# Keys of the third half by token tiles: DMA transposes and halving extrema in place of TensorE transposes and reductions, in a fused attention and feed-forward kernel

## The chip, the cores and the metric

The kernel runs on one core of a Trainium2 chip. The metric is device time in microseconds. Before the change three runs gave a median of 269.87 us (269.5 to 270.08). Engines are called TensorE (PE; its weight loads PEld), VectorE (DVE), ScalarE (ACT), GpSimd (POOL) and SyncE (SP, which only issues DMAs here).

## The reference, cut to what matters

```python
# q, k, v: (4, 8, 768, 64) float32; chunk = 32, nc = 24, top_k = 6
k_min, k_max = min / max of k over each chunk of 32 keys
ub = sum_d maximum(q * k_min, q * k_max)          # bound of each query for each chunk
ub = where(causal by chunk, ub, -1e9)
sel = the 6 chunks of largest ub, per query
scores = where(sel and causal, q @ k.T / 8, -1e9)
attn = softmax(scores) @ v                         # -> x: (3072, 512)
out = square(relu(x @ w_in)) @ w_out               # w_in (512, 2048), w_out (2048, 512)
```

## The kernel before

The sequence of each of the four batches is cut into two halves of 384 tokens, and `ORDER = ((0, 0), (1, 0), (0, 1), (1, 1), (2, 0), ...)` gives the eight (batch, half) groups, called halves 0 to 7 here; the change concerns index 2, the third, which is the second half of batch 0. Each half has four slots, one for each pair of heads, numbered s = 0 to 31; the third half is slots 8 to 11. All engine queues follow the order of the program text (a manual schedule), and each engine takes its instructions strictly in that order.

For a slot, `step_P` brings keys and queries into the form with the head dimension on partitions, `step_U` computes the chunk bounds on TensorE (tile `ub`) and picks the six largest on VectorE (MAX8, L375), `step_V` moves the choice into the code rows of the queries (transposes `qt`, copies L425), `step_E` computes scores (`ps`, L438), exponentials on ScalarE (`e`, L444) and the causal cut on GpSimd (L448), and `step_F` multiplies by v (`po`, L464), normalizes (`x`, L474) and sends x through a DMA transpose to `xT` (L478). Between these steps, `f1` takes pieces of the feed-forward of an earlier half out of a queue: up-projections (`ph`, L544, then `ht` on ScalarE and `h` on VectorE) and down-projections (`py`, L560).

There are two ways in which keys and queries are brought in.

- On TensorE, for halves 0 to 2 (`ON_PE = 3`). `load_packed` brings four tokens to a partition row in one DMA for each of k and q. `step_T` makes eight TensorE transposes for the keys of a slot (`tk`) and eight for its queries (`tq`) into PSUM. `step_T2` then has `relus_T` on ScalarE, `extrema` on VectorE (two reductions over 384 keys, L221 and L222, and one product with `hmask` into `kbd`, L223), and `place`, which copies keys (VectorE, two copies, L283) and queries (ScalarE) into `kqs`, from which the scores read.
- By DMA, for halves 3 to 7. `load_n` brings token tiles, three DMAs of 128 tokens for each of k and q. `tr` issues a DMA transpose of one tile from SP into `kqT`, `place_dma` two DMAs from there into `kqs`, and `step_K` gives six parts for VectorE that find minima and maxima of all four slots by halving (16, 8, 4, 2, 1; L326) and multiply by `hmask` (two products for each, L332). The parts are taken one at a time by `k1` at fixed places of the slot loop.

Loads are put at the ends of slots by `at(s, ...)` and drained by `go`, all on GpSimd's queue. At the ends of slots 2 to 4 stand the packed k and q of the third half, the first half of `w_out`, codes, and the second half of `w_out`. `first` and `by_sp` hold what SP issues at the start of a slot and after `step_F`.

Of the kernel before, what the change touches and what calls it, by code (L numbers as in the profile page):

```python
# [16 lines left out]
HT = 3  # L17
# [10 lines left out]

ORDER = ((0, 0), (1, 0), (0, 1), (1, 1), (2, 0), (2, 1), (3, 0), (3, 1))

ON_PE = 3

TP = 4
PP = HB // TP
# [5 lines left out]
def kernel(  # L40
# [9 lines left out]
    nc = tc.nc  # L50
# [3 lines left out]
    NP = H // 2  # L54
# [160 lines left out]
    st = {}  # L215

    def extrema(kt, s):
        b, half, p = slots[s]
        km = work.tile([128, 2, 12], BF16, tag="km", name="km")
        kv = kt.rearrange("r (j c e) -> r c j e", j=TP, c=12)  # L220
        nc.vector.tensor_reduce(km[:, 0, :], kv, axis=AX.XY, op=ALU.min)  # L221
        nc.vector.tensor_reduce(km[:, 1, :], kv, axis=AX.XY, op=ALU.max)  # L222
        nc.vector.tensor_mul(  # L223
            kbds[b % 2][:, p, :, :, 12 * half:12 * half + 12], hmask,
            km.unsqueeze(2).to_broadcast([128, 2, 2, 12]))
# [5 lines left out]
    def by_token(x):  # L231
        return x.rearrange("r (p j) -> r p j", j=TP)
# [7 lines left out]
    def step_T(s, kp, qp, ns="kq"):  # L240

        b, half, p = slots[s]
        t = st.setdefault(s, {})
        for n in ns:
            pool, tag = kp if n == "k" else qp
            x = t[n] = pool.tile([128, HB], BF16, tag=tag, name="t" + n)
            if n == "q" and s < NP:
                for hh in range(2):
                    for j in range(HT):
                        nc.tensor.matmul(  # L250
                            x[D * hh:D * hh + D, 128 * j:128 * (j + 1)],
                            lhsT=qn0[:, j, p, hh, 0:D],
                            rhs=ident, is_transpose=True, start=True, stop=True)
                continue
            for hh in range(2):
                for j in range(TP):
                    nc.tensor.matmul(
                        x[D * hh:D * hh + D, PP * j:PP * j + PP],
                        lhsT=packed(n, s // NP)[:, 2 * p + hh, D * j:D * j + D],
                        rhs=ident[0:PP, 0:PP], is_transpose=True, start=True, stop=True)  # L260

    def step_T2(s):
        relus_T(s)
        extrema(st[s]["k"], s)
        if s >= NP:
            place(s, "k", nc.vector.tensor_copy)
            place(s, "q", nc.scalar.copy)

    def relus_T(s):
# [10 lines left out]
    def place(s, n, copy, h0=0, h1=2):  # L280
        b, half, p = slots[s]
        for h in range(h0, h1):
            copy(by_token(kqs[b % 2][0:D, p, 2 * half + "kq".index(n), h, :]),  # L283
                 in_order(st[s][n][D * h:D * h + D]))
# [54 lines left out]
    F, Y, A = (psF, "ph"), (psY, "py"), (psA, "att")  # L339

    S_ = (psS, "ps")

    def step_P(s):
        if s // NP >= ON_PE:
            relus(s)
            return
        step_T(s, *((S_, Y) if s == NP + 1 else (F, Y) if s < NP + 2 else
                    (Y, S_) if s < 2 * NP + 1 else (S_, A)))
        if s >= NP + 2 and s != 2 * NP + 1:
            step_T2(s)  # L350

    def step_U(s):
# [20 lines left out]
        for j in range(j0, HT):  # L373
            for hh in range(2):
# [3 lines left out]
            (qn0[:, j0:, p, :, D:D + ncs] if s < NP else  # L378
             chosen[s % 2][:, j0:, :, 0:ncs] if s < ON_PE * NP else
             nsel[half][:, s % 2, :, j0:, 1, 0:ncs].rearrange("p h j c -> p j h c")),  # L380
# [197 lines left out]
    first = {}  # L578

    def at(s, fn, *a):  # L580
        later.setdefault(s, []).append(lambda: fn(*a))
# [15 lines left out]
        at(0, load_w_in, 1024 * g, 1024 * g + 1024)  # L597
    for j in range(HT):
        at(1, load_vt, 1, j)
    for n in "kq":  # L600
        at(2, load_packed, n, 2)
    at(4, codes, 0, 1, nc.gpsimd.dma_start)
    for g in range(2):
        at(3 + g, load_w_out, 8 * g, 8 * g + 8)
# [9 lines left out]
    by_sp = {}  # L614
    for g in range(4, 2 * B):
        for i in range(2 * HT):
            at(4 * g - (7 if g == 4 else 8) + i // HT, load_n, "kq"[i // HT], g, i % HT)
    s0 = 4 * ON_PE - 3
    for i in range(2 * HT):
        first.setdefault(s0 + i // HT, []).append((tr, ON_PE, "kq"[i // HT], i % HT))  # L620
# [80 lines left out]
    parts = []  # L701
# [5 lines left out]
    for s, (b, half, p) in enumerate(slots):  # L707
        if s < NP:
            continue
        hb = s // NP  # L710
        nb = len(BANKS[half])
        hf = nb // 2
        quota = [((4, 4, 4, 4) if hb == 1 else (8, 6, 7, 7))[p]]
        for fn, *a in first.get(s, ()):
            fn(*a)
        if (hb == ON_PE - 1 and p == 2) or (ON_PE < hb < 2 * B - 1 and p == 0):
            parts.extend(step_K(hb + 1))

        def f1():
            if quota[0] and queue:  # L720
                quota[0] -= 1
                fill(1, True)

        if s == NP:
            for n in range(hf):
                step_E(s, 0, n)
            step_F(s - 1, 0)
            step_F(s - 1, 1)
            step_P(s + 1)
            relus_T(s + 1)  # L730
            x_T(0, 1, F, (0,))
            x_copy(0, 1, 0, 1, nc.vector.tensor_copy)
            busy(8, *A)
            x_T(0, 1, F, (1,))
            x_copy(0, 1, 1, 2, nc.vector.tensor_copy)
            push(0)
            extrema(st[s + 1]["k"], s + 1)
            place(s + 1, "k", nc.vector.tensor_copy)
            place(s + 1, "q", nc.scalar.copy)
        if s == 2 * NP:  # L740
            for n in range(hf):
                step_E(s, 0, n)
            relus_T(s + 1)
            place(s + 1, "q", nc.scalar.copy)
            step_F(s - 1, 0)
            step_F(s - 1, 1)
            push(1)
            f1()
            f1()
            extrema(st[s + 1]["k"], s + 1)  # L750
            place(s + 1, "k", nc.vector.tensor_copy)
        if p == 0 and hb > 2:
            step_F(s - 1, 0)
            step_F(s - 1, 1)
            push(hb - 1)
        else:
            f1()
        if s > NP and s != 2 * NP:
            for n in range(hf):
                step_E(s, 0, n)  # L760
        k1()
        f1()
        if p == 0 and hb > 2:
            f1()
            f1()
        if hb > 1 and s != 2 * NP:
            f1()
        if hb < ON_PE:
            go(s, 2)
        for n in range(hf, nb):  # L770
            step_E(s, 0, n)
        if hb < ON_PE and p:
            k1()
        if s < NS - 2 or s + 1 == 3 * NP:
            step_U(s + (1 if hb < ON_PE else 2))
        if s + 1 == ON_PE * NP:
            step_W(s + 1)
        if hb >= ON_PE and s < NS - 2:
            step_W(s + 2)
        if ON_PE * NP - 2 <= s <= ON_PE * NP - 1:  # L780

            nc.vector.memset(
                nsel[1 - s % 2][:, :, :, :, 1, :]
                .rearrange("p i h j c -> p (i h j) c"), 0.0)
        late_f = half == 0 and hb > 2
        border = p == 0 and hb > 1
        if not border and not (late_f and p == NP - 1):
            f1()
        if p and s > NP:
            step_F(s - 1, 0)  # L790
            step_F(s - 1, 1)
        for fn, *a in by_sp.get(s, ()):
            fn(*a)
        if half == 0 and not (late_f and p in (0, NP - 1)):
            f1()
        if hb < ON_PE and p:
            k1()
        for n in range(hf):
            step_E(s, 1, n)
            if border and half and n == 0:  # L800

                f1()
        if not (late_f and p == 0):
            f1()
        if s + 1 == ON_PE * NP:
            step_P(s + 2)
            step_Q(s + 2)
        if s + 1 < ON_PE * NP:
            step_V(s + 1)
        if hb == ON_PE and p == 0:  # L810
            parts.extend(step_K(hb + 1))
        k1()
        if hb < ON_PE:
            go(s, 99)
        for n in range(hf, nb):
            step_E(s, 1, n)
        if hb >= ON_PE:
            go(s, 99)
        k1()
        if hb == ON_PE - 1 or (hb == ON_PE and p):  # L820
            k1()
        if s + 1 < ON_PE * NP:
            step_P(s + 2)
            if s + 2 == ON_PE * NP:
                step_Q(s + 2)
        if s + 1 == ON_PE * NP:
            f1()
            step_U(s + 2)
            step_W(s + 2)
        if hb >= ON_PE or s + 1 == ON_PE * NP:  # L830
            if s + 3 < NS:
                step_P(s + 3)
                step_Q(s + 3)
        f1()
        if half == 0:
            f1()
        while quota[0] and queue:
            f1()
# [40 lines left out]
```

## Time and profile before

| | |
|---|---|
| median of three runs | 269.87 us |
| profiled execution | 269.78 us |
| its span | 268.1 us |
| granted TensorE clock | 1.0 in the span's record |
| busy time in the span: TensorE / VectorE / ScalarE / GpSimd | 255.3 / 160.5 / 178.1 / 90.8 us |
| instructions | 6632 |
| bytes read from HBM / written | 27.26 / 6.29 MB |

Times in rows are microseconds from the start of the span unless marked ns. A row of the timeline gives start, length, engine, line, operation, tiles as out<-in, shape and count; brackets at the end name idle time of the engine before it and what ended it. A row by stretch gives the stretch, its length, the busy time (and count) of PE, PEld, VectorE, ScalarE and GpSimd, the granted clock, the DMA share and GB/s. Rows of the DMA view give queue (q0: the loads that GpSimd issues; q1: what SP issues), packets, MB and share; or an issue with its count, KB and the median time to landing. "SPq" marks a DMA issue on SP.

### The profile page before, as it was taken

Reading aid. Unit: us, or ns where it says so; the run is one execution under the profiler, and the core shown is the slowest. Engines: PE = TensorE matmul, PEld = TensorE weight load, DVE = VectorE, ACT = ScalarE, POOL = GpSimd, SP = SyncE. Lnnn points to the kernel's source line nnn. Section 1 sums busy time; section 2 is a strip of 40 time slices with the busy share of each in tenths; the row PEclk is TensorE's granted clock in tenths of the full one; section 3 lists DMA queues with packets and bytes.
Section 4 is the critical chain, followed back from the end, with each engine's and each line's share of the span. In section 5 each row is a group of like instructions: output and inputs, shape, how many; then the busy total and the mean of one; then the engine's idle time right before and its main releaser. Section 6 shows DMA issues by size and latency. Waiting matters only on the chain.

```text
span 268.1 us, 6632 instructions
## 1 busy us (share of the span) xinstructions
PE 255.3 (95%) x2436; PEld 157.4 (59%) x2436; DVE 160.5 (60%) x617; ACT 178.1 (66%) x399; POOL 90.8 (34%) x135
## 2 busy tenths in 40 slices
PE   7878998999999999999999999999999999999995
PEld 6566565556665566655665566745565666645543
DVE  6777999756996458546875576555863233413411
ACT  4887898688976578845575777935685688515500
POOL 8696347426911425235521543310121111000000
PEclk9999999999999999999999999999999999999999
DMA  7999999999998699999994999995532320111112
GB/s 138 153 207 211 181 218 191 120 112 151 131 170 140 137 170 149 117 177 148 191 143 118 130 166 152 157 149 134 128 98 64 61 46 16 57 39 39 39 42 78
DMA packets 116769, 33.98 MB, mean 127 GB/s; under 512 B 103680, under 2 KB 112672, under 8 KB 116736
## 3 DMA queue, kind: packets, MB, share of 16 engines
q0 software_dynamic: 64592, 13.83, 67.2%
q1 hardware_dynamic: 51200, 19.33, 37.8%
q10 hardware_dynamic: 944, 0.39, 0.6%
q8 instruction: 19, 0.31, 0.5%
q14 instruction: 14, 0.11, 0.2%
HBM read 27.26 MB, written 6.29 MB: 125 GB/s over the span
## 4 chain that ended last, share of the span: by engine, by line
PE 76%; DVE 14%; ACT 5%; issue 2%; DMA 1%; SPq 0%; ACTq 0%; DVEq 0%
PE py L560 28%; PE ph L544 24%; PE ps L438 11%; PE po L464 7%; DVE h L550 2%; ACT e L444 2%; PE ub L362 2%; DVE km L326 2%; ACT ht L548 1%; DVE m L375 1%; DMA stage<-in_q_dram 1%; PE py L532 1%; DVE kq L283 1%; DVE x L474 1%; PE idle L637 1%
## 5 line engine op out<-in xcount | busy, mean ns | idle before, releaser
L444 ACT ACTIVATE e<-ps 128x512 bf16<-128x512 f32 x192 | 96.6, 552 | 19.0 <-PE ps L438 17.9
L544 PE MATMUL ph<-xT,w_in 128*128 128x384 bf16 x512 | 98.8, 325 | 0.2 <-ACT ht L548 0.2
L560 PE MATMUL py<-w_out,h 128*128 128x512 bf16 x368 | 87.7, 379 | 0.7 <-ACT ob L566 0.5
L550 DVE TENSOR_TENSOR h<-ht 128x384 bf16<-128x384 bf16 x128 | 46.6, 374 | 56.9 <-ACT ht L548 56.3
L548 ACT ACTIVATE ht<-ph 128x384 bf16<-128x384 f32 x128 | 62.5, 501 | 26.2 <-PE ph L544 25.8
L448 POOL TENSOR_SCALAR_AFFINE_SELECT e<-e 128x384 bf16<-128x384 bf16 x64 | 34.1, 537 | 132.6 <-ACT e L444 132.5
L544 PEld LDWEIGHTS <-w_in 128*128 128x128 bf16 x512 | 47.6, 97 | 30.8 <-issue 1.4
L438 PE MATMUL ps<-kq 96*128 96x384 bf16 (+2 forms) x320 | 57.0, 277 | 1.5 <-DVE kq L414 1.0
L560 PEld LDWEIGHTS <-h 128*128 128x128 bf16 x368 | 34.9, 97 | 36.1 <-issue 1.2
L438 PEld LDWEIGHTS <-kq 96*128 96x128 bf16 x320 | 26.4, 97 | 16.1 <-issue 1.4
L566 ACT COPY ob<-py 128x512 f32<-128x512 f32 x19 | 11.1, 585 | 27.5 <-PE py L560 27.1
L464 PEld LDWEIGHTS <-e 128*128 128x128 bf16 x672 | 25.4, 98 | 4.0
L375 DVE MAX8 m<-ub 128x8 f32<-128x16 f32 (+4 forms) x160 | 16.2, 168 | 18.9 <-PE ub L369 18.5
L464 PE MATMUL po<-vn,e 128*128 128x65 bf16 x672 | 26.6, 194 | 0.0
L474 DVE TENSOR_TENSOR x<-po,r 128x384 bf16<-128x384 f32 x32 | 17.8, 557 | 1.1
L109 POOL DMA_DIRECT2D qn<-in_q_dram x15 | 13.3, 897 | 0.5 <-DVE km L326 0.2
L109 POOL DMA_DIRECT2D kn<-in_k_dram x15 | 13.4, 901 | 0.2
L362 PEld LDWEIGHTS <-qr 128*128 128x128 bf16 x160 | 8.4, 96 | 7.9 <-DVE qr L306 2.2
L326 DVE TENSOR_TENSOR km<-km 128x384 bf16<-128x384 bf16 (+3 forms) x40 | 11.7, 293 | 1.1
L362 PE MATMUL ub<-kbd,qr 128*128 128x48 bf16 (+1 forms) x160 | 9.9, 180 | 2.3 <-DVE kbd L223 0.9
L125 POOL DMA_DIRECT2D vn<-in_v_dram x12 | 10.7, 907 | 0.3 <-issue 0.3
L637 PE MATMUL idle<-ident 128*128 128x128 bf16 x97 | 8.3, 246 | 2.2 <-POOL ident masks.py:199 1.4
(69 smaller groups left out, 177.5 us busy)
## 6 DMA issues: line engine op xcount, KB each, us to landing
out_dram<-ob SPq DMA_DIRECT2D x23, 256.0 KB, 2.5
w_in<-in_moe_w_in_dram POOLq DMA_DIRECT2D x2, 1024.0 KB, 11.8
w_out<-in_moe_w_out_dram POOLq DMA_DIRECT2D x2, 1024.0 KB, 17.8
kn<-in_k_dram POOLq DMA_DIRECT2D x15, 128.0 KB, 5.6
qn<-in_q_dram POOLq DMA_DIRECT2D x15, 128.0 KB, 5.5
kq<-kqT SPq DMA_DIRECT2D x10, 192.0 KB, 3.7
vn<-in_v_dram POOLq DMA_DIRECT2D x12, 128.0 KB, 9.8
vn<-in_v_dram POOLq DMA_DIRECT2D x4, 384.0 KB, 7.9
```

The source lines that it names most:

```text
L109: nc.gpsimd.dma_start(out=nat_of(n, g)[:, DM * j:DM * j + DM].rearrange("p (h d) -> p h d", d=D), in_=rows(n, *ORDER[g], 0, H)[:, 128 * j: ...
L362: nc.tensor.matmul(ub[:, j - j0], lhsT=st[s]["qr"][:, w, 128 * j:128 * (j + 1)], rhs=kbds[b % 2][:, p, w, :, 0:ncs], start=(j == j0 and w ...
L375: nc.vector.max(out=m8[:, j, hh, :], in_=ub[:, j - j0, hh, 0:12 * half + 4 * j + 4])
L438: nc.tensor.matmul(ps[:, at:at + 128 * m], lhsT=kqs[b % 2][0:KR, p, 2 * (j // HT), hh, 128 * (j % HT):128 * (j % HT + 1)], rhs=qc(s, hh)[: ...
L444: nc.scalar.activation(e[:, 512 * n + lo:512 * n + hi], ps[:, lo:hi], ACT.Exp, scale=float(scale))
L448: nc.gpsimd.affine_select(out=d, in_=d, compare_op=ALU.is_ge, fill=0.0, base=0, channel_multiplier=-1, pattern=[[0, 3], [1, 128]])
L464: nc.tensor.matmul(po[:, hh, i, :], lhsT=t["e"][hh][:, c:c + 128], rhs=vn[b % 2][:, 2 * p + hh, j, :], start=(j == 0), stop=(j == iq))
L474: nc.vector.tensor_mul(x[:, p].rearrange("p j (h d) -> p h j d", h=2), po[:, :, :, 0:D], r.to_broadcast([128, 2, HT, D]))
L544: nc.tensor.matmul(ph[:, 0:HB], lhsT=w_in[:, ki, 128 * f:128 * (f + 1)], rhs=xT[:, ki, :], start=(ki == 0), stop=(ki == NKI - 1))
L548: nc.scalar.activation(ht, ph[:, 0:HB], ACT.Relu)
L550: nc.vector.tensor_mul(h, ht, ht)
L560: nc.tensor.matmul(py[t], lhsT=h2[hb, f][:, 128 * t:128 * (t + 1)], rhs=w_out[:, f, :], start=(f == 0), stop=(f == NFI - 1))
```

## The change

The third half's keys take the DMA way; its queries stay on the TensorE way. `K_PE = 2` marks the first half whose keys don't go over TensorE.

- The packed load of these keys becomes three loads of token tiles, one at the end of slot 2 and two at the end of slot 3, behind the packed load of the queries and ahead of `w_out`.
- SP issues three transposes at the start of slot 5, and the two placing DMAs in slot 6.
- The six parts of `step_K(2)` are queued in slot 6, and all are taken before `step_U(8)` in slot 7.
- `step_T` transposes queries alone for slots 8 to 11 (slot 8's into another PSUM bank), and `extrema` and `place` of keys fall away for them.

```diff
 ON_PE = 3
+K_PE = 2
...
-        for n in ns:
+        for n in ns[0 if s < K_PE * NP else 1:]:
...
     def step_T2(s):
         relus_T(s)
-        extrema(st[s]["k"], s)
+        if s < K_PE * NP:
+            extrema(st[s]["k"], s)
+            if s >= NP:
+                place(s, "k", nc.vector.tensor_copy)
         if s >= NP:
-            place(s, "k", nc.vector.tensor_copy)
             place(s, "q", nc.scalar.copy)
...
         step_T(s, *((S_, Y) if s == NP + 1 else (F, Y) if s < NP + 2 else
-                    (Y, S_) if s < 2 * NP + 1 else (S_, A)))
+                    (Y, S_) if s < 2 * NP else (Y, Y) if s == 2 * NP else (S_, A)))
...
-    for n in "kq":
-        at(2, load_packed, n, 2)
+    at(2, load_packed, "q", 2)
+    for j in range(HT):
+        at(2 + (j > 0), load_n, "k", 2, j)
...
+    for j in range(HT):
+        first.setdefault(5, []).append((tr, K_PE, "k", j))
+    by_sp.setdefault(6, []).append((place_dma, K_PE))
...
             f1()
             f1()
-            extrema(st[s + 1]["k"], s + 1)
-            place(s + 1, "k", nc.vector.tensor_copy)
...
+        if hb + 1 == K_PE and p == 2:
+            parts.extend(step_K(K_PE))
         if hb < ON_PE and p:
             k1()
...
         k1()
-        if hb == ON_PE - 1 or (hb == ON_PE and p):
+        if K_PE <= hb + 1 <= ON_PE or (hb == ON_PE and p):
             k1()
```

## The prediction

> **What bounds the kernel now.** I read the page first, then the busy time by stretch, then the chain of waits and each engine's timeline from 24 to 80 us, and last the DMA view over short stretches.
>
> ```profile
> PE 76%; DVE 14%; ACT 5%; issue 2%; DMA 1%; SPq 0%; ACTq 0%; DVEq 0%
> 24.00:48.00 24.00, 22.04 (x271) 14.22 (x268) 22.41 (x78) 19.70 (x48) 11.31 (x18) 1.00 1.58 194
> 48.00:78.00 30.00, 29.52 (x282) 17.47 (x282) 21.96 (x78) 24.33 (x54) 15.65 (x22) 1.00 1.95 132
> ```
>
> Over the whole span TensorE carries 76% of the chain. The change, though, touches two stretches that differ. In the second half (slots 4 to 7, about 24 to 48 us) VectorE is busy 22.4 of 24 us, and DMA is loaded as well (share 1.58; above 1, since packets overlap). In the third half (slots 8 to 11, 48 to 78 us) VectorE has 8 us free and TensorE is busy 29.5 of 30. So VectorE work taken from the third half buys little there, and VectorE work put into the second half costs its full length.
>
> **Where the new work stands.** The order of instructions shows that the first halving (it reads all of kqT's keys, so all three transposes) comes on VectorE right after the h of slot 6 and before slot 7's two copies of codes (L425).
>
> ```profile
> 41.75 0.35 DVE L550 TENSOR_TENSOR h<-ht 128x384 bf16<-128x384 bf16 x1
> 42.13 0.60 DVE L425 COPY kq<-qt 32x256 bf16<-32x256 bf16 x2
> 42.75 0.56 DVE L221 TENSOR_REDUCE km<-tk 128x12 bf16<-128x384 bf16 x1
> ...
> 44.94 0.61 DVE L550 TENSOR_TENSOR h<-ht 128x384 bf16<-128x384 bf16 x2
> ```
>
> ```profile
> 42.52 0.38 PE L438 MATMUL ps<-kq 96*128 96x384 bf16 x2
> ...
> 44.04 0.31 PE L362 MATMUL ub<-kbd,qr 128*128 128x48 bf16 x6 [0.37 <-DVE kbd L223]
> 44.19 0.17 PE L369 MATMUL ub<-cmask,ident 128*128 128x24 bf16 x1
> ...
> 48.30 0.60 PE L438 MATMUL ps<-kq 96*128 96x384 bf16 x4 [0.37 <-DVE kq L425]
> ...
> 56.21 0.37 PE L257 MATMUL tk<-ident,kn 96*64 96x96 bf16 x8
> ```
>
> VectorE reaches that place at 42.1 us. If the transposes haven't landed, it stands there, and behind it in its queue are the code copies, which slot 7's scores at 42.52 on TensorE need; behind those scores are ScalarE's exponentials and everything else. Nothing covers this wait: the whole core stops.
>
> **When the transposed keys land.** This is the decisive term. Below are the issues of the packed keys and queries today on GpSimd's timeline, and their times to landing:
>
> ```profile
> 20.26 0.84 POOL L104 DMA_DIRECT2D kn<-in_k_dram  x1
> 21.03 0.84 POOL L104 DMA_DIRECT2D qn<-in_q_dram  x1
> ...
> kn<-in_k_dram POOLq DMA_DIRECT2D x1, 384.0 KB, 13.6
> qn<-in_q_dram POOLq DMA_DIRECT2D x1, 384.0 KB, 14.8
> ```
>
> They land at 33.9 and 35.8, since the loads ahead of them in GpSimd's queue come first. In the new order the queries take the first place (33.9) and three key tiles follow. Such tiles land about 0.95 us apart (issued 67.7 to 69.5, landing 6.8 to 7.0 later):
>
> ```profile
> L109 POOL DMA_DIRECT2D kn<-in_k_dram x3: 918/918/919, 67.7 to 69.5; - x3
> DMA to landing us min/median/max: 6.8/6.9/7.0
> ```
>
> So the tiles are there at 34.8, 35.8 and 36.7, and SP, idle then, issues the transposes from 34.8 on (1.2 us each, so they follow the landings). How long transposes take while a weight load moves is shown by xT, issued at 36.5 beside w_out. Below are its time to landing, its packets over the stretch in which they ran (40 to 43.8), and the two queues from 41 to 42.5:
>
> ```profile
> xT<-x SPq DMA_TRANSPOSE x1, 7.2
> ...
> q1 hardware_dynamic: 416, 0.10, 20.9%
> ...
> q0 software_dynamic: 228, 0.23, 91.5%
> q1 hardware_dynamic: 225, 0.06, 29.8%
> ```
>
> The engines give the two queues one packet each in turn: 225 transposed packets in 1.5 us, 150 per us. The 416 packets take 2.8 us of the 7.2, so 4.4 us pass ahead of them. An xT has three blocks of 128x128, a key tile four, and there are three: 416 x 4 = 1664 packets, 11.1 us. Landing of the last: 34.8 + 4.4 + 11.1 = 50.3. This holds only while w_out moves. It does, for both halves of w_out move behind the key tiles now:
>
> ```profile
> 23.16 0.90 POOL L589 DMA_DIRECT2D w_out<-in_moe_w_out_dram  x1
> ...
> 29.07 0.56 POOL L167 DMA_DIRECT2D kq<-oneh  x1 [4.19 <-DMA w_in<-in_moe_w_in_dram]
> ```
>
> A GpSimd issue waits for the landing of the one eight before it. Two more loads stand ahead of w_out, so its first half takes the place that waits until 29.07 and starts when the keys are through.
>
> [...]
>
> The fast bound is three transposes of a quarter's keys beside 128 KB loads of small packets:
>
> ```profile
> L310 SPq DMA_TRANSPOSE kqT<-qn x3: 1217/1545/1724, 65.5 to 68.7; - x3
> DMA to landing us min/median/max: 5.8/7.1/7.2
> ```
>
> From the first issue at 65.5 to the last landing (68.7 + 7.2 at most) it is 10.4 us, so 45.2 here. I take 49.0, nearer to the w_out row, which is the same neighbour, and a little under it because the first packets run beside key tiles. The stall is 49.0 - 42.1 = **6.9 us** (3.1 to 8.2).
>
> **VectorE in the second half.** Added are the two halving trees and four products, which the fourth half's keys already go through:
>
> ```profile
> 69.13 0.55 DVE L326 TENSOR_TENSOR km<-kqT 128x768 bf16<-128x768 bf16 x1
> ...
> 70.33 0.84 DVE L326 TENSOR_TENSOR km<-km 128x384 bf16<-128x384 bf16 x2
> ...
> 73.36 0.44 DVE L326 TENSOR_TENSOR km<-km 128x96 bf16<-128x96 bf16 x2
> 73.84 0.28 DVE L332 TENSOR_TENSOR kbd<-km,hmask 128x48 bf16<-128x48 bf16 x2
> ...
> 75.16 0.56 DVE L326 TENSOR_TENSOR km<-kqT 128x768 bf16<-128x768 bf16 x1
> 75.75 1.14 DVE L326 TENSOR_TENSOR km<-km 128x384 bf16<-128x384 bf16 x4
> 76.93 0.64 DVE L332 TENSOR_TENSOR kbd<-km,hmask 128x48 bf16<-128x48 bf16 x2
> ```
>
> Together 4.4 us. Taken out is slot 8's block (two reductions, product, two copies: 42.75 to 44.94), 2.2 us. Net **+2.2**, in a stretch where VectorE is the bound. Also the last product now stands right ahead of slot 8's MAX8, so the bound matmuls (0.31 + 0.17), which ran under copies, are waited for: **+0.5**.
>
> **What the third half gains.** Three more blocks of 2.2 us leave VectorE, and 32 key transposes leave TensorE. The first and the last of the blocks, and what VectorE waits for after each:
>
> ```profile
> 50.01 0.55 DVE L221 TENSOR_REDUCE km<-tk 128x12 bf16<-128x384 bf16 x1
> ...
> 53.31 0.61 DVE L375 MAX8 m<-ub 128x8 f32<-128x16 f32 x6 [1.03 <-PE ub L369]
> ...
> 66.40 0.56 DVE L221 TENSOR_REDUCE km<-tk 128x12 bf16<-128x384 bf16 x1
> ...
> 69.96 0.44 DVE L550 TENSOR_TENSOR h<-ht 128x384 bf16<-128x384 bf16 x1 [0.29 <-ACT ht L548]
> ```
>
> After these blocks VectorE waits for another engine anyway (1.03 and 0.29 us idle), so removing it moves only idle time: 0, at most 2.2 for the last one, where the idle is short. On TensorE only slot 9's eight transposes at 56.21 lie in a stretch that TensorE bounds: **-0.3**. The other three groups sit beside VectorE's or ScalarE's work.
>
> **Moved steps that I cost at nothing.** The later w_out is first read by the down-projections of the third half, which the stall moves by 9 us. GpSimd's selects of slot 4 stand behind two more issues of 0.9; the matmuls that read them lie ahead of the stall, in a stretch where VectorE sets the pace: 0, at most 0.5. SP's xT transposes stand behind the new ones; the third half's up-projections want them, and move too. The placing DMAs wait for the transposes and land about 5.7 us after issue:
>
> ```profile
> DMA to landing us min/median/max: 5.7/5.7/5.8
> ```
>
> With the second issued 0.75 later that is 6.5 after the transposes, and slot 8's scores want them 48.3 - 42.1 + 2.7 = 8.9 after: covered by 2.4 us. The loads of the fourth half's keys now take the buffer that the transposes read, and wait for them; GpSimd's next select waits for scores that are late for the same reason, so 0.
>
> **The sum.** 6.9 + 2.2 + 0.5 - 0.3 = 9.3 us. The profiled execution took 269.78 (span 268.1); the median of the runs is 269.87, no different. 269.8 + 9.3 = 279.1. From 78 us on TensorE is busy almost throughout, so nothing later takes the delay back.
>
> **Rivals.**
> *Faster transposes.* They run at the fast bound: stall 3.1, time 275.3. For: several are outstanding at once. Against: the one-to-one turn with w_out.
> *No stall.* They land by 42.1; only the VectorE terms remain: 269.8 + 2.4 = 272.2. Needs 7.3 us from the first issue for three, which the trace shows for one alone.
> *Cold TensorE.* A stop of 6.9 us lowers TensorE's clock on top of the stall. The rows for it are the start, where the same matmul takes 113 ns apiece and later 73 or less:
>
> ```profile
> 1.43 3.17 PE L637 MATMUL idle<-ident 128*128 128x128 bf16 x28 [1.43 <-POOL ident masks.py:199]
> ...
> 5.82 0.73 PE L637 MATMUL idle<-ident 128*128 128x128 bf16 x10
> ```
>
> From 1.43 to 5.82 at most 4.4 us passed at the low rate, about half of them lost: +2, time 281.1. It decides from a stop as long as the one that made the clock low, which no row shows; after the stall VectorE sets the pace, which may hide it. [...]
> *Faster than before.* VectorE's relief in the third half reaches the end: three blocks, 6.6, less the 2.7 of the second half, 3.9 us faster, 265.9. It decides only when the transposes land by 42.1 and more than one block lies on the chain; the idle times after each block speak against it.
>
> **How the numbers follow.** Main case 0.53, faster transposes 0.20, cold TensorE 0.14, no stall 0.08, faster 0.05. The forecast is 279.1. The range 273.5 to 283 holds the first three with their bounds (275.3 less a little for idle gained in the third half; 281.1 plus a late landing) and leaves out the last two. About 0.2%, 0.5 us, is what a measurement can tell from none. Faster 0.05, same 0.02, slower 0.93.
>
> **What would show it.** Right: in the changed profile VectorE's first km of this group has an idle of several us before it, ended by the DMA kqT<-kn; TensorE's scores of slot 7 wait as long for kq L425; the three kqT<-kn issued near 35 land 7 to 15 us later; w_out is issued near 29. Wrong: those transposes landing before 42, no idle there, or a delay that is smaller at the end of the span than at slot 8's first scores.

## The result: 283.7 us, 5% slower, and above the range

The changed kernel takes 283.68 us (median of five runs, 282.52 to 284.38) against 269.87 us for the kernel before (269.5 to 270.08). The ratio is 1.0506, interval 1.0481 to 1.0531. The forecast was 279.1 us with a range of 273.5 to 283. The direction was right, the size was not. The profiled execution took 282.52 us, the shortest of the five, with a span of 280.8; against the 268.1 before, that is 12.7 us more, and these 12.7 us are what the traces have to account for. The other four executions took 0.8 to 1.9 us longer and left no trace.

From the page of the changed kernel, its span, the granted clock in 40 slices of 7.0 us, and the chain that ended last:

```profile
span 280.8 us, 6550 instructions
PEclk9999997579999999999999999999999999999999
PE 70%; DMA 10%; DVE 7%; ACT 5%; POOL 3%; issue 3%; SPq 1%; DVEq 0%; ACTq 0%; POOLq 0%
PE py L564 26%; PE ph L548 23%; PE ps L442 9%; PE po L468 7%; DMA kn<-in_k_dram 5%; DMA kqT<-kn 5%; DVE km L330 3%; ACT e L448 2%; PE ub L366 2%; ACT ht L552 2%; DVE h L554 1%; PE idle L645 1%; PE py L536 1%; POOL e L452 1%; SPq L314 1%
```

DMA held 1% of the chain before and holds 10% now, half of it the loads of the key tiles and half their transposes. The clock line has a hole in slices 7 to 9, at 42 to 63 us, that was not there before. Line numbers are two to eight higher than before: L429 is the old L425, L330 the old L326, L442 the old L438.

The new wait on VectorE's timeline after:

```profile
42.34 0.35 DVE L554 TENSOR_TENSOR h<-ht 128x384 bf16<-128x384 bf16 x1
51.06 0.56 DVE L330 TENSOR_TENSOR km<-kqT 128x768 bf16<-128x768 bf16 x1 [8.37 <-DMA kqT<-kn]
51.65 0.60 DVE L429 COPY kq<-qt 32x256 bf16<-32x256 bf16 x2
...
56.76 0.61 DVE L379 MAX8 m<-ub 128x8 f32<-128x16 f32 x6 [0.47 <-PE ub L373]
```

The same place on VectorE's timeline before:

```profile
45.58 0.61 DVE L375 MAX8 m<-ub 128x8 f32<-128x16 f32 x6
```

And TensorE's timeline after:

```profile
51.98 0.59 PE L442 MATMUL ps<-kq 96*128 96x384 bf16 x2 [8.86 <-DVE kq L429]
...
56.34 0.36 PE L366 MATMUL ub<-kbd,qr 128*128 128x48 bf16 x5 [2.24 <-DVE kbd L336]
...
56.57 1.44 PE L548 MATMUL ph<-xT,w_in 128*128 128x384 bf16 x4
...
61.39 0.60 PE L442 MATMUL ps<-kq 96*128 96x384 bf16 x4 [0.43 <-DVE kq L429]
```

VectorE stands for 8.37 us at the first halving, and TensorE's scores of slot 7 stand for 8.86 behind the copies that queue behind it. That is the stall of the prediction, at its place. But the way from the first halving to slot 8's scores is longer too: 51.06 to 61.39 is 10.33 us, where before, from the code copies at that place, 42.13 to 48.30 was 6.17. The transposes themselves, by their line, and the packets of the two queues from 42 to 43.5:

```profile
L314 SPq DMA_TRANSPOSE kqT<-kn x3: 1218/1304/1317, 35.1 to 37.9; - x3
DMA to landing us min/median/max: 8.9/12.2/13.1
```

```profile
q0 software_dynamic: 235, 0.25, 93.5%
q1 hardware_dynamic: 238, 0.05, 29.0%
```

Issued at 35.1, 36.5 and 37.9, the last landed 13.1 us later, at about 50.9. Packet for packet the two queues take turns, 238 to 235, while a packet of q0 is 1.06 KB and one of q1 0.21 KB on average. From 46 to 51 the same view has 1,076 packets of q0 and 1,072 of q1, but those of q0 then carry 0.24 KB each: the last 5 us of the wait run for the most part beside small packets, such as those of the value loads (vn) issued from 38.2, and no longer beside w_out's large ones. The turns stay one to one. GpSimd's timeline shows the loads of w_out and the wait for the transposes:

```profile
29.50 0.88 POOL L593 DMA_DIRECT2D w_out<-in_moe_w_out_dram  x1 [4.06 <-DMA w_in<-in_moe_w_in_dram]
...
33.20 0.91 POOL L593 DMA_DIRECT2D w_out<-in_moe_w_out_dram  x1
34.10 1.62 POOL L452 TENSOR_SCALAR_AFFINE_SELECT e<-e 128x384 bf16<-128x384 bf16 x3
...
51.50 1.77 POOL L111 DMA_DIRECT2D kn<-in_k_dram  x2 [8.14 <-DMA kqT<-kn]
```

### The profile page after: what moved, and what is told of

Its sections match the earlier page's. It is cut to its first block, busy times and chain, and to the rows that moved or that the text cites. A ratio compares the mean times of both kernels' runs of the same rounds, so it can differ in the third digit from the quotient of the medians.

```text
span 280.8 us, 6550 instructions
## 1 busy us (share of the span) xinstructions
PE 255.9 (91%) x2379; PEld 157.9 (56%) x2404; DVE 155.8 (55%) x611; ACT 178.3 (63%) x399; POOL 92.9 (33%) x137
## 4 chain that ended last, share of the span: by engine, by line
PE 70%; DMA 10%; DVE 7%; ACT 5%; POOL 3%; issue 3%; SPq 1%; DVEq 0%; ACTq 0%; POOLq 0%
PE py L564 26%; PE ph L548 23%; PE ps L442 9%; PE po L468 7%; DMA kn<-in_k_dram 5%; DMA kqT<-kn 5%; DVE km L330 3%; ACT e L448 2%; PE ub L366 2%; ACT ht L552 2%; DVE h L554 1%; PE idle L645 1%; PE py L536 1%; POOL e L452 1%; SPq L314 1%
## 5 line engine op out<-in xcount | busy, mean ns | idle before, releaser
L548 PE MATMUL ph<-xT,w_in 128*128 128x384 bf16 x512 | 100.7, 330 | 0.4 <-ACT ht L552 0.3
L564 PE MATMUL py<-w_out,h 128*128 128x512 bf16 x343 | 82.6, 379 | 2.2 <-ACT ob L570 0.5
L554 DVE TENSOR_TENSOR h<-ht 128x384 bf16<-128x384 bf16 x128 | 47.6, 381 | 64.0 <-ACT ht L552 63.6
L442 PE MATMUL ps<-kq 96*128 96x384 bf16 (+2 forms) x320 | 57.4, 279 | 10.6 <-DVE kq L429 9.3
L442 PEld LDWEIGHTS <-kq 96*128 96x128 bf16 x320 | 26.6, 98 | 25.7 <-issue 11.5
L570 ACT COPY ob<-py 128x512 f32<-128x512 f32 x19 | 11.1, 586 | 27.5 <-PE py L564 27.1
L111 POOL DMA_DIRECT2D kn<-in_k_dram x18 | 16.1, 898 | 9.2 <-DMA kqT<-kn 8.1
L330 DVE TENSOR_TENSOR km<-km 128x384 bf16<-128x384 bf16 (+3 forms) x48 | 13.6, 283 | 1.3
L330 DVE TENSOR_TENSOR km<-kqT 128x768 bf16<-128x768 bf16 x12 | 6.6, 551 | 8.4 <-DMA kqT<-kn 8.4
```

What stands on the lines that cost most here:

```text
L111: nc.gpsimd.dma_start(out=nat_of(n, g)[:, DM * j:DM * j + DM].rearrange("p (h d) -> p h d", d=D), in_=rows(n, *ORDER[g], 0, H)[:, 128 * j: ...
L330: nc.vector.tensor_tensor(y, x[:, :, :, 0:m], x[:, :, :, m:2 * m], op=op)
L442: nc.tensor.matmul(ps[:, at:at + 128 * m], lhsT=kqs[b % 2][0:KR, p, 2 * (j // HT), hh, 128 * (j % HT):128 * (j % HT + 1)], rhs=qc(s, hh)[: ...
L548: nc.tensor.matmul(ph[:, 0:HB], lhsT=w_in[:, ki, 128 * f:128 * (f + 1)], rhs=xT[:, ki, :], start=(ki == 0), stop=(ki == NKI - 1))
L554: nc.vector.tensor_mul(h, ht, ht)
L564: nc.tensor.matmul(py[t], lhsT=h2[hb, f][:, 128 * t:128 * (t + 1)], rhs=w_out[:, f, :], start=(f == 0), stop=(f == NFI - 1))
```

## The experiments

Each experiment is an edit of the changed kernel, where no other is named; ratios are against the kernel before, run on the same chip. The theory: the stall is the landing of the transposes beside w_out, and behind it VectorE's added work and TensorE's half clock cost the rest. The rivals were that the transposes take this long whatever else moves, and that the half clock costs nothing.

**w_out later.** Both halves of w_out are issued at the end of slot 6, behind the transposes' issue.

```diff
-        at(3 + g, load_w_out, 8 * g, 8 * g + 8)
+        at(6, load_w_out, 8 * g, 8 * g + 8)
```

> The changed kernel with both halves of w_out issued in slot 6 instead of slots 3 and 4, so that they come behind the transposes. Theory of the packet turn with w_out: the transposes still begin near 35 but only their last third meets w_out; the last lands at 43 to 46 instead of 50.9, VectorE's wait falls from 8.4 to 1 to 4 us, the clock stays up or nearly so, and the time is 274 to 277.5. Rival, that three transposes in one queue take some 16 us whatever else moves: landing stays at 48 to 51 and the time at 281 or more. Second rival: the weights come too late for the down-projections and the wait only moves there (TensorE waiting at the first py for 2 us or more).

275.88 us (274.57 to 277.87), ratio 1.0233 (1.018 to 1.0285): 7.8 us less than the change, and as expected. VectorE's wait fell to 4.08 us. The clock did not stay up: on the page it is at 8 tenths in the slice from 41.4 to 48.3 and at 5 in the next, to 55.2, and four up-projections took 1.44 us at 51.66, where four at 41.64 took 0.82. The transposes by their line, in an execution of 277.87 us:

```profile
L314 SPq DMA_TRANSPOSE kqT<-kn x3: 1211/1217/1298, 35.3 to 38.0; - x3
DMA to landing us min/median/max: 2.4/2.4/8.1
```

Two transposes that met no weight load took 2.4 us each; the third, issued at 38.0 with w_out issued at 37.7, took 8.1. So a transpose does not take long by itself. The same edit with slot 7:

```diff
-        at(3 + g, load_w_out, 8 * g, 8 * g + 8)
+        at(7, load_w_out, 8 * g, 8 * g + 8)
```

> The changed kernel with both halves of w_out issued in slot 7: nothing large moves beside the transposes. By the packet turn the last of them lands at 40 to 43, VectorE waits 0 to 0.5 us, and slot 8's scores start near 52; then w_out, issued at 43 and landing at 50 and 56, is what is late: TensorE waits 1 to 3 us at the down-projections. Time 273 to 276. If transposes are slow by themselves, the wait on VectorE stays over 5 us and the time over 280.

280.49 us (280.22 to 281.64), ratio 1.0405 (1.0372 to 1.0438). The expectation missed: the key wait was almost gone (0.75 us), but TensorE then stood for the weights. Its timeline:

```profile
43.65 0.38 PE L442 MATMUL ps<-kq 96*128 96x384 bf16 x2 [1.27 <-DVE kq L429]
...
60.59 3.57 PE L564 MATMUL py<-w_out,h 128*128 128x512 bf16 x8 [4.18 <-DMA w_out<-in_moe_w_out_dram]
```

So w_out makes the transposes slow, and w_out can't go far out of the way: it has no slack of its own. It is not alone in this: the third transpose took 5.0 us here, beside the value loads issued from 37.6, before w_out was issued at 42.4.

**TensorE kept awake.** Matmuls of a constant tile, which nothing reads, are put where TensorE waited; first ahead of slot 7's scores alone.

```diff
+        if s == 2 * NP - 1:
+            busy(140, *F)
         if s > NP and s != 2 * NP:
```

> The changed kernel with 140 more idle matmuls (128x128) on TensorE right ahead of slot 7's scores, where TensorE stands still for 8.9 us and after which its clock is at half from 46.2 to 59.8 us. They run inside the wait. If the low clock costs time on the way from the landing of the transposes to slot 8's first scores (10.3 us there, 6.2 before the change, of which 2.7 were expected from VectorE), that way falls to about 8.9 and the kernel is about 1.5 us (1 to 2.2) faster than the changed kernel, near 282. Rival: VectorE sets the pace there and the clock costs nothing; then the time stays within 0.5 us of the changed kernel's 283.7. The stall itself stays at 8 to 9 us in both.

282.69 us (282.2 to 283.38), ratio 1.0476 (1.044 to 1.0513). The stretch around slot 8's bounds, by its own row (columns as before: length, busy times, granted clock):

```profile
56.20:59.60 3.40, 3.18 (x26) 2.00 (x26) 2.01 (x12) 0.49 (x1) 0.00 (x0) 0.51 1.71 135
```

The clock was 1.00 from 46.2 to 56.2 and then fell all the same. The long wait was filled; what was left was TensorE's wait for VectorE's halving, 2.38 us for kbd, with one bound matmul of 0.18 and another 0.65 of waiting ahead of it. The way from the first halving to slot 8's scores stayed at 10.2 us (51.14 to 61.35), where the expectation had about 8.9. The median is 1.0 us below the changed kernel's, at the edge of what was expected, but the traced execution has a span 0.6 longer (281.4). This run alone settles nothing, for it left the low clock where the work is. So a second group was put ahead of slot 8's bounds:

```diff
         if s == 2 * NP - 1:
             busy(140, *F)
...
+        if s == 2 * NP - 1:
+            busy(36, *F)
         if s < NS - 2 or s + 1 == 3 * NP:
             step_U(s + (1 if hb < ON_PE else 2))
```

> The changed kernel with idle matmuls in both waits of TensorE: 140 ahead of slot 7's scores and 36 ahead of slot 8's bounds, where it waits 2.2 us for the halving. In the changed kernel 4.6 us pass from slot 8's MAX8 to its scores, 2.7 before the change. If half clock is what makes this slow (the down ph of four matmuls takes 1.44 there instead of 0.81), the clock stays full up to slot 8, this stretch falls to about 3, and the kernel is 1.3 to 2 us faster than the changed one: 281.7 to 282.4. Rival: the stretch is long because TensorE's queue had to wait for the halving and its work comes late at any clock; then 4 us or more remain at full clock and the time stays within 0.7 us of 283.7, or of the 282.7 that the first wait filled gave.

280.46 us (279.73 to 281.53), ratio 1.0397 (1.0371 to 1.0422): 3.2 us less than the change in the medians, about twice what was expected. The stretch 46.2 to 59.8 in the changed kernel:

```profile
46.20:59.80 13.60, 5.57 (x35) 3.22 (x35) 6.84 (x28) 1.85 (x4) 3.24 (x4) 0.50 2.00 119
```

and with both groups of idle matmuls:

```profile
46.20:59.80 13.60, 11.42 (x180) 9.87 (x177) 7.17 (x29) 2.75 (x7) 3.24 (x4) 1.00 1.98 133
```

VectorE's MAX8 and TensorE's scores of slot 8 in that kernel, from its two timelines:

```profile
57.21 0.61 DVE L379 MAX8 m<-ub 128x8 f32<-128x16 f32 x6 [0.39 <-PE ub L373]
```

```profile
60.31 0.60 PE L442 MATMUL ps<-kq 96*128 96x384 bf16 x4 [0.42 <-DMA kn<-in_k_dram]
```

From MAX8 to scores it is 3.10 us here, 4.63 in the changed kernel (56.76 to 61.39) and 2.72 before (45.58 to 48.30). So the half clock cost 1.5 us on this way, of the 1.9 by which it had grown. The medians differ by 3.2; the two profiled executions differ by 1.1 only, since this one had its keys 0.5 later. What makes up the rest of the 3.2 is open.

**No transposes of these keys.** `tr` is left out for the third half; halving and the placing DMAs read a part of w_in of the same shape, so the third half's selection and keys are not those of the input.

```diff
-                x = tT[hb][:, :, 0, :].rearrange("p a (c j) -> p a c j", j=CH)
+                x = w_in[:, :, 0:HB] if hb == K_PE else tT[hb][:, :, 0, :]
+                x = x.rearrange("p a (c j) -> p a c j", j=CH)
...
-    for j in range(HT):
-        first.setdefault(5, []).append((tr, K_PE, "k", j))
```

> The changed kernel without the three transposes of the third half's keys; halving and placing DMAs read a part of w_in, long there, in their stead (so the third half's selection and keys are not those of the input). Loads, VectorE's added work, placing DMAs and the order of all queues stay. What is left should be the terms of VectorE and the late selects alone: +2.2 +0.5 -0.3 and +0.6, 272.9 (272 to 274) against 269.9 before. If VectorE's added work costs more than the prediction had (the 4.2 us between landing and slot 8's scores taken whole), 274 to 275. Rival, that the loads by token tiles or the placing DMAs cost by themselves: 276 or more.

277.0 us (275.02 to 277.29), ratio 1.0252 (1.0209 to 1.0295). That is 3 us above the expected 272 to 274 and within the rival's bounds. TensorE's wait of 1.11 us for the placing DMAs, at 55.68, is of the kind that this rival named. GpSimd's and TensorE's timelines show the larger reason:

```profile
34.15 0.91 POOL L595 DMA_DIRECT2D w_out<-in_moe_w_out_dram  x1
35.05 1.61 POOL L454 TENSOR_SCALAR_AFFINE_SELECT e<-e 128x384 bf16<-128x384 bf16 x3
```

```profile
35.65 0.92 PE L470 MATMUL po<-vn,e 128*128 128x65 bf16 x12 [1.35 <-POOL e L454]
```

GpSimd's selects of slot 4 stand behind issues that wait for earlier landings. TensorE waited 1.35 us for them, and its granted clock fell (0.57 in the row of the stretch). The first halving starts at 44.90.

```profile
36.00:40.00 4.00, 3.90 (x34) 2.18 (x34) 2.48 (x8) 1.66 (x4) 1.15 (x4) 0.57 1.27 223
```

The prediction had these selects at nothing, at most 0.5. The next run puts codes and the second half of w_out behind the selects:

```diff
-    at(4, codes, 0, 1, nc.gpsimd.dma_start)
+    at(5, codes, 0, 1, nc.gpsimd.dma_start)
...
-        at(3 + g, load_w_out, 8 * g, 8 * g + 8)
+        at(3 + 2 * g, load_w_out, 8 * g, 8 * g + 8)
```

> The kernel without transposes (halving and placing read w_in), with codes and w_out's second half moved behind slot 4's selects. There the selects stood 4 us behind GpSimd's loads and slot 6 ended 2.9 us late, with the clock at half from 36.2 to 39.6. If the late selects are what cost that, the first halving starts at 42 to 42.6 instead of 44.9, the clock does not fall there, and the time is 274 to 275 (277.0 with late selects). Left are VectorE's work and what follows, about 4 us, and up to 1 us for the placing DMAs. Rival: the late start has another cause (the loads themselves); then the time stays at 276.5 or more.

274.54 us (274.07 to 276.68), ratio 1.0195 (1.0157 to 1.0234): 2.5 us less in the medians, as expected. The two kernels' executions overlap, but their traces agree with it: the halving starts 2.98 us earlier, the span is 2.8 shorter, and the clock stays up in that stretch:

```profile
36.00:40.00 4.00, 3.67 (x51) 2.51 (x51) 3.88 (x11) 3.96 (x11) 2.40 (x4) 1.00 1.24 227
```

What is left is the price without any stall. VectorE's and TensorE's timelines, and the stretch behind slot 8's bounds:

```profile
41.92 0.55 DVE L332 TENSOR_TENSOR km<-w_in 128x768 bf16<-128x768 bf16 x1
...
47.41 0.61 DVE L381 MAX8 m<-ub 128x8 f32<-128x16 f32 x6 [0.39 <-PE ub L375]
```

```profile
47.08 0.28 PE L368 MATMUL ub<-kbd,qr 128*128 128x48 bf16 x5 [2.26 <-DVE kbd L338]
...
52.92 0.60 PE L444 MATMUL ps<-kq 96*128 96x384 bf16 x4 [1.19 <-DMA kq<-w_in]
```

```profile
47.40:50.80 3.40, 3.40 (x22) 1.84 (x20) 1.95 (x10) 0.75 (x2) 0.00 (x0) 0.50 2.72 122
```

The halving starts where the code copies started before, and MAX8 comes 5.49 us later, where it was 3.45: VectorE's added work, +2.04. From MAX8 to the scores it is 5.51 instead of 2.72, with 1.19 of waiting for the placing DMAs, which in this kernel also move beside w_out (its second half was issued at 33.59, and the median to landing of the two halves is 14.1 us). The clock is at half behind the wait for the halving (2.26 us), although nothing stood still for the transposes: the half clock comes with VectorE's added work, and not with the stall alone. Idle matmuls, 36 of them ahead of slot 8's bounds, were to tell whether it is part of the price:

```diff
+        if s == 2 * NP - 1:
+            busy(36, *F)
```

> The kernel without the key transposes and with the late selects behind slot 4's (the third half's keys are still those of another tensor), and with 36 idle matmuls on TensorE ahead of slot 8's bounds, where it waits 2.26 us for VectorE's products. Theory: with no stall, VectorE's halving is what the change costs, and the half clock behind that wait (47.4 to 50.8) lies beside work that the placing DMA sets anyway (slot 8's scores wait 1.19 for it), so the clock stays up and the time hardly moves: 274 to 275 us. Rival: the clock is part of the 4.7 us that this kernel still loses against the kernel before, as it was in the kernel with the stall: 272 to 273.2.

276.65 us (273.89 to 277.15), ratio 1.0237 (1.0185 to 1.029), which overlaps with the kernel without them. TensorE's timeline in an execution of 277.15 us:

```profile
54.29 1.01 PE L444 MATMUL ps<-kq 96*128 96x384 bf16 x4 [3.28 <-DMA kq<-w_in]
```

The rival (272 to 273.2) is out. The clock does its part here too: four up-projections behind the bounds take 0.81 us, where they took 1.33, and from MAX8 to the start of slot 8's code copies it is 2.60 us (48.34 to 50.94), where it was 4.04 without the idle matmuls (47.41 to 51.45). But the scores then wait 3.28 us for the placing DMAs, so a faster TensorE has nothing to win there. These DMAs ended the wait 1.4 us later than in the other kernel's traced execution (54.29 and 52.92), and the loads of w_out took longer too, 15.2 us to landing by the median against 14.1. The idle matmuls come behind the issue of both; why the loads took longer is open.

**Reductions in place of halving.** The transposes stay, but each slot's extrema are found by two reductions over kqT at the old place, behind the code copies.

```diff
+    def extrema_T(s):
+        ...
+        nc.vector.tensor_reduce(km[:, 0, :], kv, axis=AX.X, op=ALU.min)
+        nc.vector.tensor_reduce(km[:, 1, :], kv, axis=AX.X, op=ALU.max)
...
+            extrema_T(s + 1)
...
-        if hb + 1 == K_PE and p == 2:
-            parts.extend(step_K(K_PE))
```

> The changed kernel with the halving undone: the keys still come by DMA transposes and placing DMAs, but each slot's extrema are two reductions and a product at the old place, read from the transposed keys, behind slot 7's code copies. The wait for the transposes stays (landing near 51) and the whole effect is on VectorE: 4.4 us of halving and products become 1.2 for slot 8, and TensorE no longer waits 2.2 us at the bounds. If the VectorE terms and what follows from them are worth the 4.1 us by which the way from landing to slot 8's scores grew, less slot 7's own scores that now run inside the wait, the time falls by 3 to 6 us, to 277.5 to 280.5. If only the landing counts: within 1 us of 283.7.

278.76 us (278.24 to 280.16), ratio 1.0337 (1.0312 to 1.0362), as expected. VectorE's and TensorE's timelines:

```profile
51.59 0.55 DVE L233 TENSOR_REDUCE km<-kqT 128x12 bf16<-128x384 bf16 x1 [7.31 <-DMA kqT<-kn]
```

```profile
53.16 0.40 PE L378 MATMUL ub<-kbd,qr 128*128 128x48 bf16 x6 [8.00 <-DVE kbd L235]
...
59.05 0.60 PE L454 MATMUL ps<-kq 96*128 96x384 bf16 x4 [0.95 <-DMA kq<-kqT]
```

From the first reduction to the scores it is 7.46 us, and 0.6 of code copies now run ahead of the wait: 8.06 against the change's 10.33. So halving for all four slots at once, with the clock behind it, costs 2.3 us here. The medians differ by 4.9; the two traced executions, the longest of this kernel and the shortest of the changed one, by 2.4. The shorter way brings the next wait to light, 0.95 for the placing DMA that the change covered. With the same edit, key tiles ahead of the packed queries, and codes and the second half of w_out behind slot 4's selects:

```diff
-    at(2, load_packed, "q", 2)
...
-        at(2 + (j > 0), load_n, "k", 2, j)
-    at(4, codes, 0, 1, nc.gpsimd.dma_start)
-    for g in range(2):
-        at(3 + g, load_w_out, 8 * g, 8 * g + 8)
+        at(2 + (j > 1), load_n, "k", 2, j)
+    at(3, load_packed, "q", 2)
+    at(3, load_w_out, 0, 8)
+    at(5, codes, 0, 1, nc.gpsimd.dma_start)
+    at(5, load_w_out, 8, 16)
```

> The kernel with reductions, and the loads in another order: key tiles ahead of the queries, codes and w_out's second half behind slot 4's selects. The tiles land about 2 us earlier (33 to 35), the first half of w_out still meets the transposes, the second later. Landing of the last at 45 to 47, VectorE's wait 2.5 to 4 us; the placing DMAs then land at 51 to 53, about when slot 8's scores want them. Time 272 to 275, still behind 269.9. By the rival that the transposes need 15 us whatever else moves: landing 48 to 49 and 276 or more.

277.91 us (276.97 to 279.7), ratio 1.0305 (1.0267 to 1.0343): missed. The time and the last landing (48.9) lie where the rival put them, but its reason, that the transposes need 15 us whatever else moves, is ruled out by the 2.4 us above. From the tile kqT of this kernel:

```profile
L326 SPq DMA_TRANSPOSE kqT<-kn x3: 1215/1226/1952, 31.9 to 35.2; - x3
DMA to landing us min/median/max: 8.3/10.5/13.7
```

Issued about three microseconds earlier, the transposes still took 8 to 14 us each, and the wait was 5.70. The second half of w_out, meant to come later, was still ahead of the third transpose (35.2) by an estimate: from the same place of the program it was issued at 33.59 in the kernel without transposes and with the loads behind the selects.

**The best of these together.** Both halves of w_out at slot 6, with 64 idle matmuls ahead of slot 7's scores and 36 ahead of slot 8's bounds.

> The changed kernel with both halves of w_out issued at slot 6, and with idle matmuls on TensorE: 64 ahead of slot 7's scores (where it waited 4.5 us in the kernel with w_out at slot 6) and 36 ahead of slot 8's bounds. Theory: the transposes land near 46 as there and the clock stays up, which is worth the 1.6 to 3 us that it was worth in the kernel with the stall: 272.8 to 274.3, still slower than the kernel before. Rival 1: the clock is worth nothing once the stall is 4 us: 275.5 to 277. Rival 2: stall and clock are all that the change costs beyond the landing, and the time comes within 1 us of the kernel before: 269 to 271.

Three executions took 280.64 to 281.07 us, outside every expectation, and one 275.28, just under rival 1's bounds. The expected 272.8 to 274.3 was not reached; with one execution so far from three, no ratio is given, and the run settles nothing on the price of the clock. VectorE's timeline in the profiled one, of 280.64:

```profile
50.02 0.56 DVE L330 TENSOR_TENSOR km<-kqT 128x768 bf16<-128x768 bf16 x1 [8.12 <-DMA kqT<-kn]
...
56.44 0.61 DVE L379 MAX8 m<-ub 128x8 f32<-128x16 f32 x6 [1.19 <-PE ub L373]
```

The transposes came later than in the traced execution with w_out at slot 6 alone: there the first was issued at 35.3, and the first halving started at 46.1; here none was issued before 36.0, and the first halving started at 50.02. So 0.7 us or somewhat more at the start of this race stood against 3.9 at its end. The loads were late from the start: the two loads of w_in ahead of the key tiles in the queue took 13.3 us to landing by the median, not 11.8, and they were issued long before the place of the edits. Why is open; that the execution of 275.28 had them earlier would fit, but it left no trace. From MAX8 at 56.44 the scores followed at 59.54, again 3.10 us with TensorE kept awake. No version came within 4 us of the kernel before.

## Why the prediction missed

The working against its own steps, in the profiled executions:

| step | forecast | measured |
|---|---|---|
| first halving, against the code copies before | +6.9 (42.1 to 49.0) | +8.9 (42.13 to 51.06) |
| from there to slot 8's scores | +2.2 and +0.5 | +4.16 (6.17 to 10.33) |
| third half, to the end | -0.3 | -0.4 (12.7 of 13.1 left) |
| sum | 9.3 | 12.7 |

**The landing: mechanism right, value too low.** Three transposes issued near 35 behind key tiles, one-to-one turns with w_out (238 packets against 235 from 42 to 43.5), and a landing 7 to 15 us later all came as written. The prediction's row gave 15.5 us from the first issue to the last landing (4.4 and 11.1); measured were 15.9 (35.1 to 50.9). The failing step is the choice behind it, 49.0 instead of 50.3, "a little under it because the first packets run beside key tiles". Nothing priced that discount, which is 1.3 of the 2.0 us that this term was short. The rest is the issue at 35.1 instead of 34.8 and the 0.4 us above the row; the landing at 50.9 lies over the upper bound, 50.3. That the row fits to 0.4 us is partly luck, for its two parts missed in opposite directions: no packet of SP's queue moved from 35.1 to 38.7, 3.6 us where the forecast had 4.4, and from there to the landing it was 12.2 where it had 11.1, with w_out's large packets in the way for the first part of that only.

**VectorE's work: right.** To MAX8 it is 3.45 us before and 5.70 after, 0.47 of it the wait for the bounds: +2.25, forecast 2.7. The kernel without transposes gives +2.04. Undoing the halving saves 2.3 as far as slot 8's scores, the clock included.

**The half clock: the second step that failed, a rival that should have been a term.** From MAX8 to the scores the change adds 1.9 us, and the sum had nothing there. "Cold TensorE" was set beside the main case with a chance of 0.14, as if it were another outcome. It came on top of the main case. Its condition was too narrow as well: it spoke of a stop of 6.9 us, but the clock also fell with that stop filled (2.38 us of waiting for the halving) and with no wait for transposes at all (2.26). The wait for the halving was in the forecast, as VectorE's 2.2 us, without what it does to TensorE. The doubt, "after the stall VectorE sets the pace, which may hide it", held for part of it alone: the up-projections at 56.57 take 1.44 us where four took about 0.81, VectorE waits for what follows from them, and keeping TensorE awake takes 1.5 us of the 1.9 back. With 50.3 for the landing and the rival's +2 in the sum, the forecast would have been 282.4 us, with the measured 283.68 still 1.3 above it. In the changed kernel the granted clock was 1.00 up to 46.0 and 0.50 from 46.2, about 3 us into the idle of 8.86 us. In the kernel without transposes it was down from 36.2 on behind a single wait of 1.35 us, so one length of wait does not fit both. The rival's +2 had no lowered clock behind it: at the start of the kernel before, from which it was taken, matmuls took 113 ns and later 73, but the granted clock is 1.00 in both stretches, 0 to 4 and 4 to 8 us.

**Steps costed at nothing.** In the changed kernel the late selects hold TensorE up for 0.6 us, and slot 6's last h comes 0.6 late (42.34, before 41.75); the stall hides that. In the kernel without transposes the second half of w_out is issued 0.95 later still (34.15, not 33.20), the selects with it, and there they are worth some 2.5 us, five times the bound of 0.5. The placing DMAs landed at 58.7, 2.7 us ahead of the scores, with a forecast cover of 2.4; with reductions, where the way got shorter by 2.3 us, they were waited for. The wait for the buffer, costed at 0, is real on GpSimd (8.14 us at 51.50) and coincides with VectorE's. The third half gave back 0.4 of 13.1 us: VectorE's relief there was idle time, as said.

## What to carry to other kernels

Ask of every DMA that a tight engine will wait for what else moves then, and count packets, not bytes: here 238 packets of transposes, 0.21 KB each, moved in the time of 235 packets of 1.06 KB. When a row prices a step and nothing prices a discount on it, take the row. And what follows from a wait that the forecast itself contains, such as the clock that was at 0.50 here behind a wait of 2.26 us, belongs in the same sum and not among the alternatives.

## What the runs showed of the hardware

- A 128 KB transpose took 2.4 us from issue to landing with little else moving, 5.0 us beside the value loads, and 8.9 to 13.1 us where two 1 MB loads of weights moved too.
- In the kernel with 140 idle matmuls the granted clock fell from 1.00 to 0.51 when TensorE had worked for 0.18 of the last 3 us; in the kernel without transposes it fell behind a single wait of 1.35 us (0.57 over 36 to 40). In the first of these it stayed low for 3.4 us in which TensorE was busy for 3.18; in the changed kernel it was low for 13.6 us, with TensorE busy for 5.57.
- With w_out issued at 37.7, a transpose issued 0.3 us behind it landed 8.1 us after its issue, and two issued ahead of it took 2.4 us each. In another kernel with the same order of loads the first transpose was issued at least 0.7 us later, and VectorE's wait for the last one ended 3.9 us later.
